# x of two more blocks transposed by the DMA queue, the first up step in halves, and a new set of dates for the order

## The chip, the cores and the metric

The kernel runs on one core of one Trainium2 chip. The metric is the device time of one execution in microseconds (us), the median of several runs. A profiled execution has a span (first to last instruction of the program) and its own time, which is a little longer.

## What is computed

Attention with a local window and a few global keys, and behind it a gated feed-forward layer. Batch 4, 8 heads, 768 positions, 64 elements a head; window 96, 8 global keys; 3072 tokens of 512 elements, 2048 hidden.

```python
scores = scale * np.matmul(q, k.transpose(0, 1, 3, 2))
is_global = pos[None, :] < int(n_global)
is_local = (rel >= 0) & (rel < int(n_local))
dist = np.where(is_global & ~is_local, float(n_local), np.abs(rel))
scores = scores - slopes[:, None, None] * dist          # slope 2**-(h+1) of head h
scores = np.where(is_global | is_local, scores, -1000000000.0)
a = np.exp(scores - np.max(scores, axis=-1, keepdims=True))
a = a / (np.sum(a, axis=-1, keepdims=True) + 1e-09)
x = np.matmul(a, v)                                     # heads side by side: 3072 x 512
h = x @ w_in                                            # 512 x 2048
out = (h * (1.0 / (1.0 + np.exp(-1.702 * h)))) @ w_out  # 2048 x 512
```

All data are float32. The kernel keeps the precision by splitting a factor into a high and a low half of 16 bits and adding three products (high x high, high x low, low x high).

## The kernel before

**Tiling.** The tokens are 24 blocks of 128 rows; two blocks make a chunk of 256 rows, so there are 12 chunks. Blocks 0 to 3 are the first 128 positions of each of the four batches (`EARLY = 4`, `place`); a window never leaves such a block, and they are treated apart (`prep_first`, `first`). Blocks 4 to 23 look back at the block before them (`prep`, `unit`, four units of two heads each).

**Attention of blocks 0 to 3.** `load` fetches q and k, 256 KB each. `turn` transposes them on TensorE, four float32 transposes of 128x128 each into a PSUM bank (`tq`, line 485). `taken` evicts them, scaled, to `QZ` (queries, with zeros that `clean` writes into the other half) and `KF` (keys; line 492). `scores` (lines 672 and 673) multiplies them and adds the mask, VectorE takes the maxima (line 677), a small transpose (line 680) and a copy (line 681) bring them into place, the transposed scores follow (lines 692 to 698), an exponential on ScalarE (line 710) and the products with v (line 704). `weigh_first` (lines 739 to 743) divides and writes `x` of the block.

**x for the feed-forward layer.** `finish` makes two 16-bit halves of x, transposed. For blocks under `TURN_X` TensorE transposes x into PSUM (line 763, four transposes a block), ScalarE casts the high half (line 766) and VectorE subtracts for the low half (line 767). For the others, the halves are made first, in `x16` (lines 771 and 773), and one DMA transpose on SP's queue brings both into place (line 774). `x_ready[n]` is the last of these tasks.

**The feed-forward layer.** w_in and w_out come in eight steps each (`weights(s, u)`): a load of 1 MB (line 242) and five operations of VectorE and ScalarE (lines 420 to 426) that split it into halves. For chunks 0 and 1, `up(c, s)` multiplies a chunk with a step of w_in: 24 matmuls with 256 moving columns (line 861), then tanh and the gate on ScalarE and VectorE (lines 870 to 873). `down(c, s)` multiplies with w_out and accumulates in PSUM (line 969). Chunks 2 to 11 use `up_two` and `down_two`, a scheme with seven in place of eight products over two steps (line 901), for which `twist` prepares sums of the weights and `sums` sums of x.

**What sets the order.** Every piece of work is a task: the engines it can run on with a duration each, the tasks it comes after, the buffers it uses, and a due time. `Work.order` runs once when the program is built. It passes due times back along the dependencies, adds the entry of `NUDGE` for the task's tag (`tag` for engines, `tag` with an "l" for tasks of SP's queue), and then plays the engines and the DMA queue through in a planned time: a free engine takes the ready task with the earliest due time whose buffers are free. A task isn't looked at until `AHEAD` = 24 us before it is due, or until its own `soon`. A DMA is planned as 1.95 us of latency, its duration on the one queue and 0.9 us to land. The result is a fixed order of instructions for each engine; on the chip each engine works in that order and waits for semaphores. Durations and dates have no other effect than on this order and on the choice of the engine. Where TensorE would have nothing to do in the first `WARM` = 50 us of planned time, the planner puts in a filler, a matmul of ones that nobody reads (`spare`, line 1147); fillers use the ring of banks `r_h`, and so do the transposes `tq` of blocks 1 to 3 and the up steps.

**Buffers.** A `Ring` has a number of buffers under one tag. A `Buf` takes the next one; in rings that are not `loose` they are taken in the order in which they were declared. PSUM has eight banks: `r_s` 1, `r_pv` 1, `r_h` 2, `r_y` 4. `r_x16` has one buffer, which holds the masks (`mk`) at first.

**Masks.** From two small integers (window and number of global keys) a matmul (`cs`, line 392) and some VectorE operations make the masks: `M1` for a block's own keys (line 385, 128x128), then `m2` and `M2` for the keys of the block before (lines 375 to 377, and 383 or 385 with 128x256), which are first used by block 4.

Of the kernel before, what the change touches and what calls it, by code (L numbers as in the profile page):

```python
# [8 lines left out]
F32 = mybir.dt.float32  # L9
# [10 lines left out]
P = 128  # L20
# [8 lines left out]

NUDGE = {"M2": -8.8, "T2": 21.9, "T3": 11.2, "block1": 2, "block10u2": -2.7, "block10u2l": -0.5,  # L30
# [37 lines left out]
NG = 8  # L68
SKIP = 24
EARLY = 4  # L70

FIRST = 4
LAST = 0.9365
TURN_X = 4
WARM, GAP = 50.0, 0.5
AHEAD = 24.0
BACKLOG = 3.0
TWO = 3
LAT = 0.2
MM128, MM256, MM512, MM64, FP128, FP65, TURN = 0.056, 0.109, 0.216, 0.029, 0.264, 0.21, 0.11  # L80
# [165 lines left out]
def kernel(  # L246
# [11 lines left out]
    nc = tc.nc  # L258
# [1105 lines left out]
```

## Time and profile before

| | us |
|---|---|
| median of 3 runs | 588.26 (587.92 to 588.53) |
| the profiled execution | 587.09 |
| its span | 585.2 |
| TensorE (PE) busy | 577.2 |
| VectorE (DVE) busy | 497.1 |
| ScalarE (ACT) busy | 461.5 |

An engine is counted as busy from the start to the end of each of its instructions; matmuls overlap in the pipeline and their ends are modelled, so that a following matmul's start tells more than an end. PEld is the loading of weights, which overlaps with matmuls. "Idle" is the time of an engine ahead of an instruction, and the profile names what ended it. SP only issues DMAs and waits; its transfers run on 16 DMA engines that all queues share. A row of a timeline merges instructions of one kind that follow each other.

### The profile page before, as it was taken

The page shows a single profiled execution, that of the slowest core. Times are in us where ns is not written, and L with a number is a line of the kernel's source. Part 1 is how long each engine was busy: PE and PEld are TensorE (multiplying, and loading weights), DVE is VectorE, ACT ScalarE, POOL GpSimd, SP SyncE. Part 2 cuts the span into 40 slices and gives each one's busy share as a digit, 9 for nine tenths or more (in the row PEclk, how much of TensorE's full clock was granted, in tenths as well). Part 3 has the DMA queues.
Part 4 walks back from the last instruction along what each step waited for, and adds up shares of the span by engine and source line. Part 5 has one row for each costly group of instructions (what it writes and reads, how often), then busy time and mean ns, then how long its engine had stood idle before and what let it go on. Part 6 is the DMA issues. An engine that isn't in the chain of part 4 may idle for free. (4 is left out here: it accounts for less than half of the span.)

```text
span 585.2 us, 16904 instructions
## 1 busy us (share of the span) xinstructions
PE 577.2 (99%) x6744; PEld 435.0 (74%) x6744; DVE 497.1 (85%) x1180; ACT 461.5 (79%) x1086; POOL 3.7 (1%) x14
## 2 busy tenths in 40 slices
PE   8999999999999999999999999999999999999997
PEld 5886766677668678778679767777777866876896
DVE  7898999999999999888899699889889878775462
ACT  6778899898678979888798798788987878874351
POOL 2000000000000000000000000000000000000000
PEclk9999999999999999999999999999999999999999
DMA  9998998987667787989999998999998899970101
GB/s 259 299 295 215 312 227 244 207 202 144 166 145 147 146 154 163 215 162 198 226 183 194 200 222 207 200 219 189 247 202 189 203 204 227 196 182 19 37 2 41
DMA packets 268265, 109.57 MB, mean 187 GB/s; under 512 B 249300, under 2 KB 249812, under 8 KB 268180
## 3 DMA queue, kind: packets, MB, share of 16 engines
q1 hardware_dynamic: 268032, 108.30, 83.3%
q8 instruction: 54, 0.88, 0.7%
q14 instruction: 31, 0.25, 0.1%
q10 hardware_dynamic: 148, 0.13, 0.1%
HBM read 57.67 MB, written 6.29 MB: 109 GB/s over the span
## 5 line engine op out<-in xcount | busy, mean ns | idle before, releaser
L969 PE MATMUL y<-w,g 128*128 128x512 f16 (+1 forms) x1248 | 264.9, 363 | 0.2
L969 PEld LDWEIGHTS <-g 128*128 128x128 f16 x1248 | 118.0, 98 | 106.3 <-DVE g L873 1.0
L901 PEld LDWEIGHTS <-w 128*128 128x128 f16 x1728 | 101.4, 98 | 3.9
L615 ACT ACTIVATE p<-p,NM 128x232 f32<-128x232 f32 x160 | 76.3, 479 | 9.4 <-DVE NM L605 9.3
L901 PEld LDWEIGHTS <-T 128*128 128x128 f16 x1296 | 76.8, 98 | 5.2 <-issue 0.2
L861 PE MATMUL h<-xT,w 128*128 128x256 f16 x576 | 67.2, 273 | 0.2 <-DVE t L871 0.2
L605 DVE CUSTOM_DVE_ANT_0 p<-s,mm 128x232 f32<-128x232 f32 x160 | 57.5, 393 | 9.8 <-PE s L599 9.5
L861 PEld LDWEIGHTS <-w 128*128 128x128 f16 x576 | 55.4, 98 | 8.1 <-DVE t L871 0.3
L942 DVE SCALAR_TENSOR_TENSOR g<-t,g 128x512 f16<-128x512 f32 x72 | 49.0, 685 | 11.8 <-ACT g L941 11.6
L620 DVE TENSOR_TENSOR hl<-p,hl 128x464 f16<-128x464 f32 x80 | 50.7, 635 | 5.1 <-ACT hl L619 4.8
L941 ACT ACTIVATE g<-t 128x512 f16<-128x512 f32 x72 | 44.9, 628 | 12.4 <-PE y L969 8.5
L933 ACT ACTIVATE t<-h 128x512 f32<-128x512 f32 (+1 forms) x72 | 35.8, 517 | 18.3 <-DVE h L909 16.6
L619 ACT CAST hl<-p 128x464 f16<-128x464 f32 x80 | 46.0, 575 | 2.2 <-DMA pt<-hl 0.8
L909 DVE TENSOR_TENSOR h<-pb,h 128x256 f32<-128x256 f32 x72 | 28.4, 418 | 19.6 <-PE pb L901 17.3
L901 PE MATMUL pa<-xS,T 128*128 128x128 f16 x648 | 44.8, 219 | 0.0
L599 PEld LDWEIGHTS <-QK 128*128 128x128 f16 x640 | 36.5, 98 | 5.8 <-DVE NM L605 1.7
L934 DVE SCALAR_TENSOR_TENSOR t<-t,h 128x512 f32<-128x512 f32 (+1 forms) x72 | 38.4, 550 | 2.3 <-ACT t L933 2.0
L599 PE MATMUL s<-QK 128*128 128x128 f16 x320 | 38.2, 219 | 0.0
L901 PE MATMUL pa<-xT,w 128*128 128x128 f16 x540 | 37.5, 219 | 0.0
L901 PE MATMUL pb<-xS,w 128*128 128x128 f16 x540 | 37.5, 219 | 0.0
L632 PE MATMUL pv<-VR,pt 128*128 128x64 f16 x288 | 34.5, 193 | 0.0
L631 PE MATMUL pv<-VR,pt 128*128 128x64 f16 x288 | 34.5, 193 | 0.0
(186 smaller groups left out, 1030.2 us busy)
## 6 DMA issues: line engine op xcount, KB each, us to landing
ws<-in_moe_w_in_dram SPq DMA_DIRECT2D x8, 1024.0 KB
ws<-in_moe_w_out_dram SPq DMA_DIRECT2D x8, 1024.0 KB, 5.7
raw<-in_q_dram SPq DMA_DIRECT2D x24, 256.0 KB, 4.2
raw<-in_k_dram SPq DMA_DIRECT2D x24, 256.0 KB, 5.3
QK<-QK SPq DMA_DIRECT2D x40, 128.0 KB, 5.4
raw<-in_v_dram SPq DMA_DIRECT2D x20, 256.0 KB, 3.2
out_dram<-yo SPq DMA_DIRECT2D x20, 256.0 KB
ws_00again<-in_moe_w_in_dram SPq DMA_DIRECT2D x8, 512.0 KB, 3.8
```

Of the source, the lines that this page charges most:

```text
L599: nc.tensor.matmul(sp()[:, j, lo:hi], d["QK"]()[:, 0, h, :], K[:, 1 + z, h, P - (hi - lo):], start=(z == 0), stop=(z == 1), skip_group_che ...
L605: nc.vector.tensor_tensor_reduce(out=pr()[:, j, :], in0=sp()[:, j, :], in1=m, scale=-1.0 / SC, scalar=3.0e38, op0=ALU.add, op1=ALU.min, ac ...
L615: ex.append(add({"ACT": 0.473}, lambda e, j=j: nc.scalar.activation(pr()[:, j, :], pr()[:, j, :], AF.Exp, bias=NM[:, n, hs[j]:hs[j] + 1], ...
L619: t4 = add({"ACT": 0.5}, lambda e: nc.scalar.copy(hl()[:, 0, :, SKIP:], pr()), ex, [pr, hl])
L620: t5 = add({"DVE": 0.55}, lambda e: nc.vector.tensor_sub(hl()[:, 1, :, SKIP:], pr(), hl()[:, 0, :, SKIP:]), [t4], [pr, hl])
L861: nc.tensor.matmul(ph()[:, fi, :], w1(s, cc, z, fi), X[:, y, cc, :], start=(j + cc == 0), stop=(j == 2 and cc == NCC - 1))
L901: nc.tensor.matmul(o()[:, fi], w, x()[:, y * NCC + 2 * k + cc, t], start=(first and fi + j + cc == 0), stop=(last and j + cc == 3), skip_g ...
L933: t1 = add({"ACT": 0.06 + 0.22 * w}, lambda e: nc.scalar.activation(o(), src(), AF.Tanh, scale=0.851 / (SX * SW)), after, srcs)
L934: return add({"DVE": 0.08 + 0.265 * w}, lambda e: nc.vector.scalar_tensor_tensor(o(), o(), 1.0, src(), ALU.add, ALU.mult), [t1], srcs)
L941: t4 = add({"ACT": 0.53}, lambda e, g=g, tt=tt: nc.scalar.mul(g()[:, 0], tt(), SG / (SX * SW)), u, [tt, g])
L942: t5 = add({"DVE": 0.61}, lambda e, g=g, tt=tt: nc.vector.scalar_tensor_tensor(g()[:, 1], tt(), SG / (SX * SW), g()[:, 0], ALU.mult, ALU.s ...
L969: nc.tensor.matmul(y(), part(zg, f), w2(s, z, f % 2)[:, m], start=(begin and f + j == 0), stop=(end and j == 2 and f == 2 * len(steps) - 1 ...
```

## The change

- `TURN_X` goes from 4 to 2: x of blocks 2 and 3 (chunk 1) goes through `x16` and the DMA transpose.
- `HALVES = 1`: `up(0, 0)` is issued as four tasks in place of two, each with 12 matmuls of 128 columns, one for each block of the chunk and each half `fi` of the step; a task waits only for its own block's `x_ready`.
- `turns`: the transposes `tq` of block 1 get the banks `r_y[0, 1]` and `r_pv`; those of block 0 keep `r_y[1, 0]` and `r_y[1, 1]`.
- `clean`: the zeros of blocks 1 and 2 are POOL's, those of blocks 0 and 3 ScalarE's (before: 0 and 1 ScalarE's, 2 and 3 POOL's), with other due times; block 3's is not looked at before 12 us of planned time.
- `m2` and `M2` are not looked at before 12 us of planned time.
- The planner's durations of loads, DMA transposes, `counts` and the small matmul `cs` are other ones.
- All entries of `NUDGE` are replaced.
- The first buffers of `r_VF`, `r_KG` and `r_pr` are allocated ahead of the others.

```diff
-NUDGE = {"M2": -8.8, "T2": 21.9, "T3": 11.2, "block1": 2, "block10u2": -2.7, "block10u2l": -0.5,
...
+NUDGE = {"T0": -17.4, "T1": -25.4, "again": 11.6, "block10u0": -0.2, "block10u3": 16.8, "block11u0": 1.5,
...
-TURN_X = 4
+TURN_X = 2
...
+HALVES = 1
...
-    m1 = add({"DVE": 0.55}, counts, [m0], want=0.0)
-    m1 = add({"PE": 0.12}, lambda e: nc.tensor.matmul(cs(), each, one, start=True, stop=True), [m1], [cs])
+    m1 = add({"DVE": 1.0}, counts, [m0], want=0.0)
+    m1 = add({"PE": 0.6}, lambda e: nc.tensor.matmul(cs(), each, one, start=True, stop=True), [m1], [cs])
...
+    for t in (m2, *M2):
+        t.soon = 12.0
...
-        t0 = add({"SP": 2.75}, lambda e: load_weights(nc, ws(), w_in, w_out, s, u), bufs=[ws])
+        t0 = add({"SP": 2.5}, lambda e: load_weights(nc, ws(), w_in, w_out, s, u), bufs=[ws])
...
-        return [add({"SP": 1.2 if n < 2 and 2 not in parts else 1.35}, lambda e, z=z: nc.sync.dma_start(
+        return [add({"SP": 0.95}, lambda e, z=z: nc.sync.dma_start(
...
-        zero = add({"ACT": 1.2} if n < 2 else {"POOL": 1.2}, clean, bufs=[QZ], want=-10.0 if n < 2 else 1e9)
+        zero = add({"POOL": 1.1} if n in (1, 2) else {"ACT": 1.25}, clean, bufs=[QZ], want=(-10.0, 0.0, 1e9, 1e9)[n])
+        if n == 3:
+            zero.soon = 12.0
...
-            tq = Buf(r_y[1, z] if n == 0 else r_h, [P, NU, P], F32, f"tq{n}_{z}")
+            tq = turns.get((n, z)) or Buf(r_h, [P, NU, P], F32, f"tq{n}_{z}")
...
-            add({"SP": 1.2 if n < 2 else 1.35}, lambda e: nc.sync.dma_start(
+            add({"SP": 1.0}, lambda e: nc.sync.dma_start(
...
-        t3 = add({"SP": f * 2.8}, lambda e: nc.sync.dma_start_transpose(
+        t3 = add({"SP": f * 2.1}, lambda e: nc.sync.dma_start_transpose(
...
-        t6 = add({"SP": 0.7 * ns}, lambda e: nc.sync.dma_start_transpose(pt(), hl().rearrange("p a h w -> p (a h w)")),
+        t6 = add({"SP": 0.55 * ns}, lambda e: nc.sync.dma_start_transpose(pt(), hl().rearrange("p a h w -> p (a h w)")),
...
+    turns = {(n, z): Buf(r, [P, NU, P], F32, f"tq{n}_{z}") for n, z, r in
+             ((0, 0, r_y[1, 0]), (0, 1, r_y[1, 1]), (1, 0, r_y[0, 1]), (1, 1, r_pv))}
...
-        t4 = add({"SP": 1.4}, lambda e: nc.sync.dma_start_transpose(xT[c]()[:, :, t, :], x16().rearrange("p a m -> p (a m)")),
+        t4 = add({"SP": 1.1}, lambda e: nc.sync.dma_start_transpose(xT[c]()[:, :, t, :], x16().rearrange("p a m -> p (a m)")),
...
-        def mms(e, fi):
+        def mms(e, fi, at):
...
-                    nc.tensor.matmul(ph()[:, fi, :], w1(s, cc, z, fi), X[:, y, cc, :],
+                    nc.tensor.matmul(ph()[:, fi, at], w1(s, cc, z, fi), X[:, y, cc, at],
...
-        t1 = ups[c, s] = [add({"PE": 12 * MM256}, lambda e, fi=fi: mms(e, fi), [x_ready[2 * c], x_ready[2 * c + 1], W_ready[s, 0]],
-                  [ph, xT[c], WT[s, 0]], want + 1.3 * fi) for fi in range(2)]
+        pieces = [(slice(0, TC), (0, 1))] if c or s >= HALVES else [(slice(t * P, t * P + P), (t,)) for t in range(2)]
+        t1 = ups[c, s] = [add({"PE": 12 * MM256 / len(pieces) + 0.018 * (len(pieces) - 1)}, lambda e, fi=fi, at=at: mms(e, fi, at),
+                              [*(x_ready[2 * c + t] for t in ts), W_ready[s, 0]], [ph, xT[c], WT[s, 0]], want + 1.3 * fi)
+                          for at, ts in pieces for fi in range(2)]
...
+    for r in (r_VF, r_KG, r_pr):
+        r.line[0]()
```

73 rows, old and new, of the table NUDGE are left out of this document.

## The prediction

> **What bounds the kernel now.** I read the page first, then busy time by stretches with the filler matmuls of line 1147 apart, then TensorE's timeline up to 51 us, and last the groups that the change touches. From the page:
>
> ```profile
> span 585.2 us, 16904 instructions
> PE 577.2 (99%) x6744; PEld 435.0 (74%) x6744; DVE 497.1 (85%) x1180; ACT 461.5 (79%) x1086; POOL 3.7 (1%) x14
> ```
>
> TensorE is busy for 99% of the span. The chain of waits says nothing here (one piece, the last ScalarE instruction), so I look for the stretches in which TensorE does no useful work. Columns: stretch, length, busy time (and instructions) of PE, PEld, DVE, ACT, POOL, clock, DMA share, GB/s. Behind it, the same for the filler matmuls alone.
>
> ```profile
> 0.00:4.91 4.91, 3.58 (x11) 1.22 (x11) 2.79 (x15) 3.29 (x5) 3.68 (x14) 1.00 0.63 143
> 4.91:14.57 9.66, 8.87 (x82) 6.75 (x82) 8.27 (x29) 6.72 (x12) 0.00 (x0) 1.00 1.07 317
> 14.57:21.44 6.87, 6.87 (x65) 6.30 (x62) 5.58 (x12) 5.37 (x7) 0.00 (x0) 1.00 0.90 198
> 21.44:26.27 4.83, 3.73 (x38) 3.08 (x38) 4.70 (x11) 3.30 (x7) 0.00 (x0) 1.00 1.01 384
> 26.27:45.00 18.73, 18.73 (x178) 16.66 (x176) 17.04 (x27) 13.93 (x20) 0.00 (x0) 1.00 1.00 302
> 45.00:60.00 15.00, 15.00 (x105) 10.15 (x104) 13.69 (x22) 12.07 (x14) 0.00 (x0) 1.00 0.85 214
> 60.00:130.00 70.00, 69.28 (x638) 48.80 (x636) 68.19 (x140) 64.88 (x137) 0.00 (x0) 1.00 0.96 240
> 130.00:581.30 451.30, 451.10 (x5644) 342.01 (x5642) 376.85 (x929) 351.45 (x889) 0.00 (x0) 1.00 0.82 170
> ...
> 4.91:26.27 21.36, 1.85 (x7) 0.59 (x6) 1.00 1.00 294
> ```
>
> So the time splits into four: 4.91 us ahead of the first useful matmul; a start up to 26.27, in which 1.85 us is filler and 0.79 + 1.10 = 1.89 us is idle, 3.74 us in all; a body of 555 us in which TensorE idles 0.72 + 0.20 = 0.92 us; and a tail of 3.9 us behind the last matmul. Only three things can make the kernel faster: less TensorE work, less of the 4.91 + 3.74, less of the 0.92. The edits reach no further than that, about 7 us; there is no such floor under a loss. The second thing to see is VectorE: 17.04 of 18.73, then 68.19 of 70 us busy. It converts the weights, and what is put on it late stays late for long.
>
> **The change part by part.** TensorE's timeline around the start (start us, us, instruction):
>
> ```profile
> 5.21 0.66 PE L485 MATMUL tq<-ident,raw 128*128 128x128 f32 x4
> 5.71 0.81 PE L1147 MATMUL idle<-idle 128*128 128x512 bf16 x3
> 6.36 0.60 PE L485 MATMUL tq<-ident,raw 128*128 128x128 f32 x4
> 7.79 0.22 PE L672 MATMUL s<-hl,QZ 128*128 128x128 bf16 x1
> 8.69 0.60 PE L485 MATMUL tq<-ident,raw 128*128 128x128 f32 x4
> 9.17 0.38 PE L1147 MATMUL idle<-idle 128*128 128x512 bf16 x1
> 10.54 0.22 PE L672 MATMUL s<-hl,QZ 128*128 128x128 bf16 x1 [0.31 <-ACT hl L492]
> 22.75 0.65 PE L763 MATMUL tx<-ident,x 128*128 128x128 f32 x4 [0.27 <-DVE x L743]
> 25.27 0.66 PE L485 MATMUL tq<-ident,raw 128*128 128x128 f32 x4 [0.83 <-ACT QZ L492]
> 26.27 1.47 PE L861 MATMUL h<-xT,w 128*128 128x256 f16 x12
> 27.58 0.27 PE L680 MATMUL aux<-ident,top 128*8 128x128 f32 x1
> 47.39 0.60 PE L763 MATMUL tx<-ident,x 128*128 128x128 f32 x4
> 47.82 2.75 PE L969 MATMUL y<-w,g 128*128 128x512 f16 x12
> 50.41 2.78 PE L861 MATMUL h<-xT,w 128*128 128x256 f16 x24
> ```
>
> *x of blocks 2 and 3 by the queue.* Four transposes occupy TensorE from 47.39 to 47.82, 0.43 us; two blocks are 0.87 us. The last filler is the one at 9.17, so what is freed there is used by the next matmul: −0.87 (bounds 0, if it only turns into idle time, and −0.87). On ScalarE and VectorE almost nothing changes, since a cast and a subtraction stay, from SBUF in place of PSUM:
>
> ```profile
> L766 ACT CAST xT<-tx x4: 580/585/585, 20.0 to 48.0; 128x512 f16<-128x512 f32 x4
> L771 ACT CAST x<-x x13: 602/614/620, 96.7 to 526.1; 128x512 f16<-128x512 f32 x13
> L773 DVE TENSOR_TENSOR x<-x,x x20: 678/684/693, 98.2 to 527.1; 128x512 f16<-128x512 f32 x20
> L774 SPq DMA_TRANSPOSE xT<-x x20: 1233/1314/3387, 108.0 to 527.8; - x20
> DMA to landing us min/median/max: 4.3/4.9/5.7
> 46.42 0.21 DVE L743 TENSOR_TENSOR x<-aux,sm 128x64 f32<-128x64 f32 x1
> 49.44 0.67 DVE L767 TENSOR_TENSOR xT<-tx,xT 128x512 f16<-128x512 f32 x1
> ```
>
> What changes is when chunk 1 is there. Now x of block 3 is written at 46.42 + 0.21 = 46.63 and its transposed halves at 50.11; the up step that begins at 50.41 fits to that, and I take it for chunk 1's first. By the queue, 0.61 + 0.68 + 4.9 = 6.2 us lie between, so from the same x it would be 52.8, 2.7 us later. Queued behind the two transposes on SP are weight and key loads, 1.3 us of issuing for each; SP and the DMA engines have room there (the DMA share is 0.85 in 45 to 60). I cost the 2.7 us at nothing because attention of block 3 can be put ahead of chunk 0's second and third up steps, 2 x 2.62 us of TensorE work that the trace has in front of it; if the new order doesn't, this is the first rival's loss.
>
> *First up step in halves.* Twelve matmuls of 256 columns take 27.58 − 26.27 = 1.31 us, so the step 2.62. In halves it is 48 matmuls of 128 columns. Of lines 672 and 673 sixteen such matmuls, each with a weight load of its own, run from 7.79 to 8.69, 0.056 us each: 48 x 0.056 = 2.69, +0.07 (that each loads its own weights excludes a dearer price). Its first half needs block 0 alone. The waits of 0.27 and 0.83 us at 22.75 and 25.27, 1.10 us, can then be covered by 1.3 us of up work, if block 0's x and the first weight are ready by 22:
>
> ```profile
> L426 DVE SCALAR_TENSOR_TENSOR w<-wa,w x5: 1212/1215/1227, 16.3 to 39.1; 128x1024 f16<-128x1024 f32 x5
> 20.57 0.69 DVE L767 TENSOR_TENSOR xT<-tx,xT 128x512 f16<-128x512 f32 x1 [0.70 <-ACT xT L766]
> 8.62 1.28 DVE L677 TENSOR_REDUCE top<-s 128x4 f32<-128x512 f32 x2
> 9.81 1.29 DVE L385 TENSOR_SCALAR mm<-mk 128x256 bf16<-128x256 f32 x6
> 9.14 0.72 ACT L383 ACTIVATE mm<-mk 128x256 bf16<-128x256 f32 x2
> ```
>
> They are: the first of the five conversions up to 50 us ends at 16.3 + 1.2 = 17.5, the halves of x at 20.57 + 0.69 = 21.26. −1.1 (bounds 0 and −1.1).
>
> *Masks later, own banks, zeros on other engines, true durations.* These go together: they decide how the remaining 4.91 + 2.64 us shrink. ScalarE does 0.72 us of masks for block 4 and later (line 383) just ahead of the eviction that the scores at 10.54 wait for; not before 12 us in the planner's time, they leave that wait. VectorE's maxima (line 677) start at 8.62, behind three mask operations, while the first four heads' scores (half of the sixteen products) are through near 8.24; they move up a little. Block 1's first transposes no longer share banks with the fillers. With loads costed at 0.95 us and not 1.2, block 0's keys are taken about 0.6 us earlier than 6.36. I take −0.8 of the 2.64 and −0.3 of the 4.91 (bounds 0 and −2.6; 0 and −1.2). Block 0's products now also wait for a bank that block 1's transposes hold; that bank is read by 10.5, and these products start at 14.57, so it costs nothing, with 4 us of cover. The 1.29 us of line 385 and some 0.8 us ahead of it move into a stretch in which VectorE has 18.73 − 17.04 = 1.69 us free: bounds 0 and +2.1 on the weights, taken as 0 because TensorE has chunk 1's steps to do meanwhile. One zero fill moves from ScalarE to POOL and one the other way, off the path.
>
> The new costs are near what the queue does. A weight load is 1,048,576 bytes, a load of q, k or v 262,144:
>
> ```profile
> 23.00:28.00 5.00, 4.17 (x44) 3.58 (x43) 4.18 (x8) 3.88 (x6) 0.00 (x0) 1.00 1.03 410
> 30.00:31.50 1.50, 1.50 (x15) 1.21 (x14) 1.50 (x3) 1.50 (x2) 0.00 (x0) 1.00 1.11 253
> ```
>
> At 410 GB/s a weight takes 2.56 us (now costed 2.5, before 2.75); at 253 GB/s a load takes 1.04 (now 0.95). The Trainium skill speaks against the new figure: on its page "DMA: Bandwidth & Descriptors", section "Where 436 GB/s comes from", the memory side binds a transfer from HBM at about 358 GB/s. By that a weight takes an estimated 2.93 us, the five weights that are converted before 50 us would be 5 x 0.43 = 2.1 us later than costed, and the sum would end 2.1 us higher. The row of 410 GB/s disagrees with it, and the measurement decides.
>
> *Dates anew.* All the dates by which the order is made are replaced. This adds and removes no work; it can only change idle time. The body has 0.92 us of it, so the gain ends at −0.9. A loss has no row; nearest is the worst stretch of before, 0.72 us in 70, and four times that, +2.9 us, is my bound above. I take 0, since with costs nearer to the traced ones I see no reason for a worse body.
>
> **Sum:** −0.87 + 0.07 − 1.1 − 0.8 − 0.3 + 0 = −3.0 us. The profiled execution took 587.09, its span and 1.9 us around it: 584.1. The median of the runs shown is 588.26, 1.17 above it; on that scale the forecast is **585.2**, with a range of its own of 583.0 to 587.0.
>
> **The rivals.** *Chunk 1 comes late (slower).* TensorE reaches the step at 50.41 some 3.0 us earlier, at 47.4, and finds chunk 1 landed only at 52.8 if block 3's x stays at 46.63: 5.4 us idle, −3.0 + 5.4 = +2.4, 590.7. For it: only five weights are converted by then (the row of line 426), so chunk 0's work is used up. Against it: attention of block 3 can go in front, which costs nothing. It decides from the x of block 3: as early as 41.2 the gain is whole, later than 44.2 it is gone, and from 45.4 on the kernel is slower by over 0.2%. By the Trainium skill's page "TensorE: Matmul & The Clock Gate", section "HAM oscillation — how this bites in real kernels", idle gaps of over about 3.4 us also halve the clock for a while; the longest gap behind the first useful matmul is 0.83 us and the clock 1.00, so no run shows it.
>
> *VectorE takes it back (no change).* TensorE arrives 3 us earlier at 60 to 130 us, where VectorE is 97% busy, and waits for scores and conversions there: idle grows from 0.7 to about 3.5 us, time 588.0. For it: that stretch's waits are on VectorE (the row below), and the masks moved 2 us of VectorE work towards it. Against it: later blocks' attention can give way.
>
> ```profile
> PE s L599 <- DVE NM L605: 0.5, 2, 0.3
> ```
>
> *The start shrinks more.* All of the 3.74 us and 0.9 of the 4.91 go: −0.8 − 3.7 − 0.9 = −5.4, 582.8. Against it: block 0's chain of evictions leaves TensorE little to do before 12 us.
>
> *The change doesn't do what it says.* The freed 0.87 us and the halves only turn into filler, which the planner may place up to 50 us: −0.3 − 0.8, 587.2. Filler behind 10 us would show it; before has none there.
>
> **How the numbers follow.** The forecast has 0.56, the larger gain 0.08, VectorE 0.13, filler 0.07, late chunk 0.16. This measurement can tell about 0.2%, 1.2 us, from no change: 587.1 to 589.4. The forecast's own range and the larger gain lie below it; of filler 0.03 does too. Faster 0.67, same 0.17, slower 0.16. The range, 582.4 to 589.2, reaches over the larger gain and over the two cases of no change, and leaves out most of the late chunk and 0.04 below.
>
> **What would show it.** Right: fillers and idle time between the first useful matmul and 26 us fall from 3.7 to under 2; the first 128-column up matmuls run near 20 us; line 763 has 8 instructions, not 16; block 3's x is written before 42; idle time in 60 to 130 us stays near 0.7. Wrong: a wait of TensorE for the transposed x between 45 and 55 us, or waits on VectorE of over 3 us behind it, would each overturn the sum.

## The result, and the profile after

The kernel with the change takes 605.08 us (600.92 to 607.76, six runs); the kernel before, on the same chip, 588.39 (587.44 to 589.43). The ratio is 1.0277, 95% interval 1.0241 to 1.0314: 16.7 us slower, where 585.2 was forecast and 589.2 was the upper end of the range. The profiled execution took 603.95 us.

From the page of the profile after:

```profile
span 602.2 us, 16916 instructions
PE 579.8 (96%) x6757; PEld 434.8 (72%) x6757; DVE 496.7 (82%) x1175; ACT 462.4 (77%) x1091; POOL 3.7 (1%) x14
q1 hardware_dynamic: 270144, 108.82, 82.3%
```

Nearly the same work, 17.0 us longer: the last ScalarE instruction, which reads the last matmul, starts at 598.29, before at 581.37. The windows after, cut where those of before were cut (first useful matmul, up step of chunk 0, and so on), with the fillers' own window row last:

```profile
0.00:4.72 4.72, 3.39 (x8) 1.28 (x9) 2.73 (x15) 2.54 (x3) 3.69 (x14) 1.00 0.60 137
4.72:26.30 21.58, 18.05 (x154) 14.55 (x153) 17.94 (x47) 16.01 (x27) 0.00 (x0) 1.00 1.01 314
26.30:45.00 18.70, 18.57 (x199) 16.27 (x199) 17.20 (x28) 14.32 (x20) 0.00 (x0) 1.00 1.04 274
45.00:60.05 15.05, 12.81 (x82) 7.92 (x81) 12.07 (x19) 10.88 (x15) 0.00 (x0) 1.00 1.12 275
60.05:130.00 69.95, 67.65 (x596) 47.66 (x595) 65.19 (x122) 60.67 (x118) 0.00 (x0) 1.00 0.87 211
130.00:598.30 468.30, 459.33 (x5722) 347.07 (x5722) 381.60 (x949) 357.51 (x912) 0.00 (x0) 1.00 0.81 168
...
4.72:26.30 21.58, 1.94 (x6) 0.49 (x5) 1.00 1.01 314
```

TensorE's idle time (length less the first busy figure) is 3.53 us in the start, where it was 1.89; then 0.13, 2.24, 2.30 and 8.97, 13.6 us in the body, where it was 0.92. That is 14.4 of the 17.0 us; the other 2.6 stand in TensorE's busy figure. An estimate of mine fits that: the trace has 32 gaps between matmuls, before 11, and a matmul of 128 columns ahead of a gap is counted with its whole 0.22 us, where the next one would start after 0.056; 21 x 0.16 = 3.4, less some 0.8 us of work that the change takes away. The loss has no one place: it is spread over the body.

What TensorE waits for, in the view of its waits (line <- what released it: us in total, times, longest):

```profile
PE pv L636 <- DMA pt<-hl: 6.4, 10, 1.1
PE h L869 <- DVE t L881: 1.3, 1, 1.3
PE h L869 <- DMA xT<-x: 1.1, 1, 1.1
...
PE s L605 <- DMA QK<-QK: 0.7, 1, 0.7
```

First come waits for `pt`, the exponentials that the DMA queue brings back transposed (line 627). The view of that tile gives what all engines that use it waited for; of its 15.0 us after, 6.4 are matmuls and 8.6 are TensorE's weight loads, which overlap with matmuls. Here is its row after; before, this list holds no DMA, only the second row:

```profile
  DMA pt<-hl: 15.0, 22
```

```profile
  PE sT L698: 2.1, 4
```

So data that the order counted on come late from the queue. Direct waits of matmuls for a DMA (`pt` 6.4, x 1.1, queries and keys 0.7, values 0.3) are 8.5 of the 13.6 us; the others name VectorE or ScalarE, and how many of these go back to a late transfer wasn't followed. What a late transfer does beyond its own wait is seen at chunk 1 (VectorE's, SP's and TensorE's timelines after):

```profile
53.10 0.21 DVE L751 TENSOR_TENSOR x<-aux,sm 128x64 f32<-128x64 f32 x1
54.50 0.69 DVE L424 TENSOR_SCALAR w<-ws 128x1024 int32<-128x1024 int32 x1 [1.18 <-DMA ws<-in_moe_w_in_dram]
55.11 1.22 DVE L430 SCALAR_TENSOR_TENSOR w<-wa,w 128x1024 f16<-128x1024 f32 x1
56.24 0.69 DVE L781 TENSOR_TENSOR x<-x,x 128x512 f16<-128x512 f32 x1
...
56.95 1.23 SPq L782 DMA_TRANSPOSE xT<-x  x1
...
60.05 3.22 PE L869 MATMUL h<-xT,w 128*128 128x256 f16 x28 [1.13 <-DMA xT<-x]
```

Block 3's x is written at 53.31, but the subtraction for its low half starts only at 56.24 (line 781): VectorE's order has a weight's first operation (line 424) ahead of it, and that stands 1.18 us for its load. The transpose goes out at 56.95, and TensorE, which had nothing to do with that weight, waits 1.13 us at 60.05.

### The profile page after: what moved, and what is told of

Read it like the earlier page. It is cut to its first block, busy times and chain, and to the rows that moved or that the text cites. A ratio compares the mean times of both kernels' runs of the same rounds, so it can differ in the third digit from the quotient of the medians.

```text
span 602.2 us, 16916 instructions
## 1 busy us (share of the span) xinstructions
PE 579.8 (96%) x6757; PEld 434.8 (72%) x6757; DVE 496.7 (82%) x1175; ACT 462.4 (77%) x1091; POOL 3.7 (1%) x14
## 5 line engine op out<-in xcount | busy, mean ns | idle before, releaser
L869 PE MATMUL h<-xT,w 128*128 128x256 f16 (+1 forms) x600 | 68.5, 268 | 4.3 <-DVE t L881 1.3
L943 ACT ACTIVATE t<-h 128x512 f32<-128x512 f32 (+1 forms) x72 | 36.0, 516 | 18.7 <-DVE h L919 17.9
L636 PE MATMUL pv<-VR,pt 128*128 128x64 f16 x288 | 34.2, 193 | 5.6 <-DMA pt<-hl 5.3
L636 PEld LDWEIGHTS <-pt 128*128 128x128 f16 x320 | 29.2, 98 | 12.1 <-DMA pt<-hl 8.6
```

Source lines behind the costliest of these rows:

```text
L636: nc.tensor.matmul(o, ph, V[:, 0, h], start=(s == 0), stop=False, skip_group_check=True)
L869: nc.tensor.matmul(ph()[:, fi, at], w1(s, cc, z, fi), X[:, y, cc, at], start=(j + cc == 0), stop=(j == 2 and cc == NCC - 1))
```

## The experiments

**How they are read.** The kernel's `order` gives a planned time for each task when the program is built, and so a planned end of the last matmul. That is no time of a chip, but it says what the order counts on. On the chip that end is taken as the start of ScalarE's last instruction less 0.1 us (in the kernel before 581.37 − 0.1 = 581.3; planned 581.0). Chip less plan is called slip. The kernel before has a slip of 0.3 us, the changed kernel one of 598.2 − 584.2 = 14.0. My theory after the traces: the order counts on more than the queue gives (MARGIN below). Its rivals: the new set of dates is at fault, or the changed structure, or SP's issuing.

| kernel | planned end | on the chip | slip | median us | ratio to before (95%) |
|---|---|---|---|---|---|
| before | 581.0 | 581.3 | 0.3 | 588.4 | |
| after | 584.2 | 598.2 | 14.0 | 605.1 | 1.028 (1.024 to 1.031) |
| e1 change, no dates | 580.1 | 614.2 | 34.1 | 623.2 | 1.060 (1.057 to 1.064) |
| e2 before, new DMA durations | 583.7 | 604.3 | 20.6 | 611.3 | 1.040 (1.037 to 1.043) |
| e3 before, no dates | 584.3 | 587.1 | 2.8 | 593.4 | 1.009 (1.006 to 1.012) |
| e4 change, old durations and dates | 587.7 | 591.9 | 4.2 | 598.2 | 1.017 (1.014 to 1.020) |
| e5 before, short transposes | 583.5 | 589.3 | 5.8 | 595.4 | 1.013 (1.010 to 1.016) |
| e6 before, short loads | 584.2 | 599.4 | 15.2 | 606.4 | 1.033 (1.030 to 1.036) |
| e7 change, old durations, no dates | 585.6 | 591.2 | 5.6 | 597.2 | 1.014 (1.011 to 1.017) |
| e8 as e1, fewer bytes | 580.1 | 604.7 | 24.6 | 608.8 | 1.033 (1.027 to 1.038) |
| e9 before, short q, k, v | 585.9 | 604.6 | 18.7 | 611.0 | 1.038 (1.035 to 1.041) |
| e10 change, old durations, dates searched | 581.9 | 592.9 | 11.0 | 598.7 | 1.017 (1.015 to 1.019) |
| e11 the same, searched with a margin | 582.5 | 593.2 | 10.7 | 598.8 | 1.016 (1.014 to 1.019) |
| e12 change, longer durations, no dates | 595.9 | 594.3 | −1.6 | 599.9 | 1.020 (1.016 to 1.023) |
| e13 before, dates searched | 581.1 | 589.8 | 8.7 | 594.6 | 1.011 (1.007 to 1.015) |
| e14 change, all DMAs x1.15, dates searched | 588.2 | 589.7 | 1.5 | 596.2 | 1.014 (1.011 to 1.016) |
| e15 before, all DMAs x1.15, dates searched | 587.4 | 589.7 | 2.3 | 595.5 | 1.013 (1.011 to 1.014) |

"No dates" is `NUDGE = {}`. The six durations are those of the weights (`t0`), of q, k and v (two places) and of the DMA transposes `t3` (queries and keys), `t6` (`pt`) and `t4` (x). Differences below are against runs of the kernel before on the same chip (587.8 to 589.0 us).

**Are the dates at fault, or the durations?** e1 is the changed kernel with

```diff
-NUDGE = {"T0": -17.4, "T1": -25.4, "again": 11.6, ...
+NUDGE = {}
```

> The changed kernel with no dates of its own (NUDGE empty): queue transposes, halves, banks, masks and the new durations stay. The order's own planned end of the last matmul is 580.1 us, for the changed kernel it is 584.2 and for the kernel before 581.0; on the chip those two ended at 598.3 and 581.3. Theory MARGIN (the new, shorter DMA durations leave the plan without slack, so that in-order engines stand at DMAs that land after their planned time): about as many body waits as in the changed kernel, end 8 or more us past the plan, median 592 to 600. Theory DATES (this one set of dates is at fault): the end is within 3 us of the plan, body idle below 3 us, median 586 to 589. Theory STRUCTURE (x of chunk 1 by the queue, halves and banks cost it): waits for xT between 45 and 60 us and a median near 590 whatever the dates.

It is slower still, 623.18 us, 23 above the range that MARGIN gave: that is 34.6 us over before, the change 16.7. So with these durations the new dates gain 17.9 us over none. The plan of e1 (e8 has the same) is the shortest of all, 580.1, and misses by the most. The tile `pt` in it:

```profile
  DMA pt<-hl: 35.7, 23
```

e2 is the kernel before, its dates too, with the new values of the six durations alone:

```diff
-        t0 = add({"SP": 2.75}, lambda e: load_weights(nc, ws(), w_in, w_out, s, u), bufs=[ws])
+        t0 = add({"SP": 2.5}, lambda e: load_weights(nc, ws(), w_in, w_out, s, u), bufs=[ws])
-        return [add({"SP": 1.2 if n < 2 and 2 not in parts else 1.35}, ...      # q, k: 0.95;  v: 1.0
-        t3 = add({"SP": f * 2.8}, ...                                           # 2.1
-        t6 = add({"SP": 0.7 * ns}, ...                                          # 0.55
-        t4 = add({"SP": 1.4}, ...                                               # 1.1
```

> The kernel before, its dates and structure kept, with only the planner's DMA durations (loads 0.95 and 1.0, weights 2.5, transposes 2.1, 1.1 and 1.1) taken from the change; no instruction differs but the order. Planned end of the last matmul 583.7 us. Theory MARGIN: end 6 or more us past the plan, median 595 to 602, TensorE waits for pt, QK or VR by DMA of over 4 us. Theory DATES: within 3 us of the plan, median 589 to 593. Theory STRUCTURE: as DATES.

611.26 us, 22.7 more than before and 9 above MARGIN's range, though only the order is another (with it the engine of some operations, and the fillers). The wait for `pt` comes first among TensorE's waits in e2, as in the changed kernel:

```profile
PE pv L630 <- DMA pt<-hl: 5.5, 9, 1.5
PE pa L901 <- ACT h L917: 3.2, 4, 1.4
```

e3 takes the dates from the kernel before and leaves its durations:

```diff
-NUDGE = {"M2": -8.8, "T2": 21.9, "T3": 11.2, ...
+NUDGE = {}
```

> The kernel before with its old, longer DMA durations and no dates (NUDGE empty). Planned end of the last matmul 584.3 us. Theory MARGIN: as with the kernel before, the end is within 2 us of the plan, median 590 to 593, hardly a wait for a DMA. Theory DATES: within 3 us of the plan too if no dates are harmless, but far behind it (over 6 us) if it is dates that keep DMAs from being late.

593.42 us: the dates of before are worth 4.9 us, and without them the plan still holds to 2.8 (MARGIN said 2, and 590 to 593 us; both are passed by less than 1). Both kernels without dates, the one slips 2.8 and the other 34.1 us, so the lack of fitted dates alone doesn't make an order slip.

**What is left of the change without the durations?** e4 is the change with the six durations and the dates of before; e7 with the six durations of before and no dates.

```diff
 e4: the six durations and NUDGE of the kernel before, in the changed kernel
 e7: the six durations of the kernel before, and
+NUDGE = {}
```

> The changed kernel's structure (queue transposes for blocks 2 and 3, halves, banks, masks, zeros, the durations of the two small mask operations) with the old DMA durations and the old dates. Planned end of the last matmul 587.7 us. Theory MARGIN: within 2.5 us of the plan, median 594 to 597, hardly a wait for a DMA behind 60 us. Theory STRUCTURE: 4 or more us past the plan, with waits for xT at 45 to 60 us. Theory DATES: within 3 us of the plan.

> The changed kernel's structure with the old DMA durations and no dates; planned end of the last matmul 585.6 us. It differs from the kernel before without dates (planned 584.3, on the chip 587.2, median 593.4) by the structure alone, and from the changed kernel without dates (planned 580.1, on the chip 614.3, median 623.2) by the six DMA durations alone. Theory MARGIN: within 5 us of the plan, median 592 to 598, and 25 us or more below the run with the new durations. Theory STRUCTURE: 8 or more us past the plan, waits for xT or for VectorE of over 4 us before 60 us, median above 600.

598.15 and 597.17 us; the dates of before do nothing for the changed kernel. Both slips are larger than MARGIN said (4.2 for 2.5, 5.6 for 5), and e4's is one that STRUCTURE named, though TensorE has no wait for a DMA of x in it. Giving the old durations back takes 25.6 us off e1 (34.6 and 9.1 over before), and the tile `pt` falls to

```profile
  DMA pt<-hl: 5.0, 10
```

These four make a path from before to after, each step one edit: dates of before taken out +4.9 (e3), the other parts of the change +4.2 (e7), the new durations +25.6 (e1), the new dates −17.9 (after). That they add up to 16.7 is no test, since each is a difference of two neighbours. And it is one path of several. By the runs e13 and e10 below, which have searched dates, it reads: other dates for the kernel before +6.9 (e13), the other parts of the change with dates searched in the same way +2.9 (e10), from there to the change, with its durations and its own dates, +7.0. So the new durations cost 22.7 us in the kernel before, with its dates, and 25.6 in the changed one without dates; but of the 16.7 us, with dates that go with them, their part may be as little as 7.

**Which durations?** On the kernel before, with its dates: e5 shortens the three transposes alone, e6 the loads of weights, q, k and v, e9 those of q, k and v.

```diff
 e5
-        t3 = add({"SP": f * 2.8}, ...
+        t3 = add({"SP": f * 2.1}, ...
-        t6 = add({"SP": 0.7 * ns}, ...
+        t6 = add({"SP": 0.55 * ns}, ...
-        t4 = add({"SP": 1.4}, ...
+        t4 = add({"SP": 1.1}, ...
 e6
-        t0 = add({"SP": 2.75}, ...
+        t0 = add({"SP": 2.5}, ...
 e6 and e9
-        return [add({"SP": 1.2 if n < 2 and 2 not in parts else 1.35}, ...
+        return [add({"SP": 0.95}, ...
-            add({"SP": 1.2 if n < 2 else 1.35}, ...
+            add({"SP": 1.0}, ...
```

> The kernel before with its dates, and of the new durations only those of the DMA transposes (2.1, 1.1, 1.1 in place of 2.8, 1.4, 1.4 us); nothing but the order differs. Planned end of the last matmul 583.5 us. With all new durations (the run before this one) the kernel ended at 604.1, 20.4 past its plan. Theory TRANSPOSES (the 256-byte packets of transposes are what the queue can't do in the planned time): 12 or more us past the plan, median above 601. Theory LOADS (q, k, v and weights are): under 6 us past it, median below 596.

> The kernel before with its dates, and of the new durations only those of the loads (weights 2.5 in place of 2.75, q, k and v 0.95 and 1.0 in place of 1.2 and 1.35 us). Planned end of the last matmul 584.2 us. Theory TRANSPOSES: under 6 us past the plan, median below 597. Theory LOADS: 12 or more us past it, median above 602.

> The kernel before with its dates, and of the new durations only those of q, k and v (0.95 and 1.0 in place of 1.2 and 1.35 us); weights and transposes keep the old ones. Planned end of the last matmul 585.9 us. All loads short: planned 584.2, on the chip 599.5, 15.3 past it. Theory QKV (a load of 256-byte packets is what is underrated, 68 of them through the body): 10 or more us past the plan, median above 602. Theory WEIGHTS (the sixteen of 1 MB ahead of 110 us): under 6 us past it, median below 599.

595.44, 606.41 and 610.99 us: +7.3, +18.3 and +22.0. The loads of q, k and v alone make as much of the loss as all six together (22.7), so the parts don't add up; the new figure for a weight isn't needed for it (with it, e6 is shorter than e9). Nor does the sum of what a plan asks of the queue rank the slips: it is 418.0 us in e5, 423.8 in e6 and 427.8 in e9, while they slip 5.8, 15.2 and 18.7. It matters which transfers are planned too short. In e9 TensorE waits for `pt` again, and for queries and keys from the queue:

```profile
PE pv L630 <- DMA pt<-hl: 6.5, 5, 2.5
...
PE s L599 <- DMA QK<-QK: 2.9, 2, 2.1
```

**Is it the queue's bytes, or SP's issuing?** SP needs 1.23 us or more to issue a transpose (1.26 in the median for `pt`, in e1), and it issues in order too. e8 has e1's order, task for task, and as many DMAs; only the 32 second loads of weights, from which sums of squares are formed, fetch 64 KB in place of 512 KB each.

```diff
-    nc.sync.dma_start(ws.rearrange("p (c f) t -> p c (f t)", c=n), ...
+    nc.sync.dma_start(ws[:, 0:few], words[0:P, 0:2 * few].rearrange("p (f t) -> p f t", t=2))     # few = 64
```

> The changed kernel without dates (median 623.2, planned end 580.1, real 614.0; TensorE idle 5.3 us in 265 to 400 and 11.2 in 400 to 530, 16.5 together, of which 13.8 is waits for pt) with one edit that leaves its order as it is: the 32 second loads of the weights (512 KB each, from 265 us on) bring 64 KB each, and the check that reads them works on those; so 14 of 110 MB and seven eighths of that check are left out, while the instructions, their number and their lengths on ScalarE, VectorE and SP stay. Theory BYTES (the queue can't move what the plan asks of it in the planned time): the DMA share in 265 to 530 falls from 0.94 to about 0.75, idle there from 16.5 to under 5 us, median 604 to 612. Theory ISSUE (it is the time that SP takes to issue a DMA, 1.26 us a transpose and about 0.57 a load, and the latency of each, that the plan misses): idle there stays above 13 us, median 618 or more.

608.83 us, 13.6 nearer to before than e1. The windows of e1 and then of e8 in which those loads lie:

```profile
265.00:400.00 135.00, 129.67 (x1666) 97.34 (x1664) 111.08 (x281) 113.15 (x291) 0.00 (x0) 0.99 0.94 194
400.00:530.00 130.00, 118.85 (x1542) 88.61 (x1540) 104.54 (x263) 102.73 (x269) 0.00 (x0) 1.00 0.94 203
```

```profile
265.00:400.00 135.00, 129.84 (x1701) 97.73 (x1699) 113.14 (x290) 114.02 (x294) 0.00 (x0) 1.00 0.82 152
400.00:530.00 130.00, 129.99 (x1683) 97.32 (x1682) 113.19 (x285) 109.99 (x291) 0.00 (x0) 1.00 0.74 158
```

In 400 to 530 us TensorE's idle time falls from 11.15 to 0.01 us, with the DMA share from 0.94 to 0.74. In 265 to 400 us it stays (5.33 and 5.16), though the share falls there too. So in the second window it is the time that transfers take on the shared queue, not the number of issues, which is the same; for the first this leaves it open, and the idle time of 5.2 us over both is just above the 5 that BYTES named.

**Does more room on the queue take the slip away?** e12 is e7 with the six durations some 15% longer:

```diff
-        t0 = add({"SP": 2.75}, ...                    +3.15
-        q and k 1.2, v and later blocks 1.35          +1.4, 1.55
-        t3, t6, t4: 2.8, 0.7, 1.4                     +3.2, 0.8, 1.6
```

> The change with no entries in NUDGE and the six DMA durations of the kernel before made about 15% longer (weights 3.15, q, k and v 1.4 and 1.55, transposes 3.2, 0.8 and 1.6 us); nothing of the work differs. The order's own plan ends its last matmul at 595.9 us, against 580.1 with the new durations and 585.6 with those of before (both without dates), where the chip ended 34 and 5.7 us behind the plan. MARGIN (an order that asks the queue for more than it gives slips, because each engine keeps its order behind a late DMA): a third dose, so the slip falls to 3 us or less, TensorE's waits for pt (the exponentials brought back transposed) to under 1 us in sum (16.2 and 1.6 in those two), median between 601 and 606 us. BOUND (the DMA engines themselves are what cannot go faster, whatever the order asks): the waits on DMAs stay as with the durations of before, and the median is within 1.5 us of 597. SCATTER (the slip has nothing to do with the durations; any order without fitted dates misses by some amount): a slip anywhere between 5 and 30 us, median 608 to 632.

The slip is gone, the chip is 1.6 us ahead of the plan, and neither the waits of TensorE nor the tile `pt` list a wait for `pt` any more. The median of 599.87 lies 1.1 below the range given for MARGIN, for the chip beat the plan. So three doses of the same structure without dates, planned shorter, as before, and longer, slip 34.1, 5.6 and −1.6 us. The room has its own price: the plan is 10.3 us longer than e7's, the time 2.7. How much room it is shows against the trace: the plan of e12 asks 520.4 us of the queue, which took 0.802 x 598.3 = 480, so it has 8% more than needed, where e7's has 466.3 for 0.837 x 595.3 = 498, 6% less.

**Why do searched dates not hold?** With the old durations, dates were found by altering `NUDGE` at random and keeping what made the plan shorter: for the plan as it is (e10), and for the mean of the plans with DMAs at 1.0 and 1.15 times their durations (e11). The edit is another `NUDGE` in e7.

> The changed kernel's structure (x of blocks 2 and 3 by the queue, halves, banks, masks) with the old DMA durations and dates searched anew for the shortest planned end under these durations: last matmul planned at 581.9 us, against 584.2 of the changed kernel and 581.0 of the kernel before. Theory BYTES (an order made with the queue's real load keeps its plan): on the chip within 6 us of the plan, median 589 to 595, at least 10 below the changed kernel. Theory STRUCTURE (queue transposes, halves and banks lose whatever the order): 10 or more past the plan, median above 598. If the structure brings what was forecast, 588 or less.

> As the run before, but the dates are searched for the mean of two plans, one with the old DMA durations and one with all of them 15% longer; built with the old durations, last matmul planned at 582.5 us. Theory BYTES, with slack worth having: fewer waits for DMAs than in the run before, within 3 us of the plan, median 588 to 592. Theory STRUCTURE: as the run before, above 598.

Both missed what BYTES said and fall where STRUCTURE put them: slips of 11.0 and 10.7, and 598.7 and 598.8 us, no better than with no dates (+9.7 and +9.8; e7 +9.1). Two causes were open, the changed structure and the fitting. e13 puts dates searched as in e10 on the kernel before; e14 and e15 plan every DMA of SP 1.15 times as long and search dates under that, for the changed structure and for that of before.

```diff
 e14, e15, in Work.order
-                t, us = best, best.on[e]
+                t, us = best, best.on[e] * (1.15 if e == "SP" else 1.0)
```

> The kernel before with its own durations and another set of NUDGE, found as for e10_change_old_durations_new_search (dates altered at random, kept where the order's own plan came out shorter). The plan ends its last matmul at 581.1 us, as the dates of before do (581.0). STRUCTURE (the 11 us by which the changed kernel missed its plan there come from the changed structure): here the plan holds as it did for before, slip under 3 us, median 588 to 591. FITTED (a plan made as short as it will go by its dates misses on the chip, whatever the structure; that the dates of before hold theirs comes from more than the plan): slip 7 to 15 us, median 595 to 603.

> The change, durations of before, every DMA planned 1.15 times as long, and dates searched for the shortest plan under these longer DMAs; it ends its last matmul at 588.2 us. MARGIN: with room on the queue even a searched plan holds: slip under 3 us, TensorE's waits for pt under 1 us in sum, median 592 to 598. FITTED without regard to the queue: slip 7 to 15 us as in e10, median 602 to 610. In neither case does it beat the kernel before (588.4).

> The kernel before with every DMA planned 1.15 times as long and dates searched for the shortest plan under that; it ends its last matmul at 587.4 us, 0.8 ahead of e14_change_longer_durations_new_search. MARGIN: slip under 3 us, median 591 to 597. STRUCTURE (the changed structure costs something by itself): e14 is longer than this one by more than 3 us; if the structure is neutral, by 0 to 2 us.

e13 slips 8.7 us on the structure of before, whose own dates give as short a plan (581.1 and 581.0) and slip 0.3. Its median, 594.62, is 0.4 below FITTED's range, yet far from STRUCTURE's 588 to 591: fitting to the plan alone can be enough for a slip of this size. (It is one set of dates; another could slip more or less. Some 2.8 of the 8.7 us are a lower clock of TensorE after early waits, as the last section works out.) With the longer DMAs the searched plans hold, 1.5 and 2.3, in the ranges given. And e14 is 0.8 us longer than e15, within the spread of their runs (594.4 to 596.9 and 594.8 to 595.8): with room on the queue no cost of the changed structure is seen, where it was 4.2 without dates, and no gain in either. Here are TensorE's two longest waits in e13, for values of a global key and for `pt`, both from the queue, and then the two longest in e14, where no DMA is among the waits:

```profile
PE pv L594 <- DMA VR<-VG: 2.1, 1, 2.1
PE pv L594 <- DMA pt<-hl: 1.4, 3, 0.7
```

```profile
PE s L568 <- DVE NM L574: 2.6, 3, 1.3
PE s L568 <- DVE QKover L515: 1.7, 1, 1.7
```

Open is what the dates of before have that searched ones lack; the plan doesn't show it, and how they were found isn't on record. No version came below the kernel before.

## Why the prediction was wrong, step by step

**The step that failed** is "The new costs are near what the queue does", and with it "Dates anew", taken as 0 and bounded by +2.9. The durations were taken as estimates that get better when they come nearer to a traced one. e2 shows what they are (22.7 us lost by them alone): an order that counts on shorter transfers asks for data sooner than they come, and each engine stands in its fixed order behind them. e13 shows that dates too can't be put at nothing: other ones cost the kernel before 6.9 us. The body's idle time went from 0.92 us to 13.6 in the changed kernel; four times the worst stretch of before was no bound, since a stretch of before says nothing of an order that asks for more. How the 16.7 us divide between durations and dates stays open, as the two paths above show.

The two rows were also read wrongly. 410 and 253 GB/s are rates of 5 and 1.5 us in which the queue had one kind of work (by the packet records, 745 packets of 2 and 4 KB and almost no others in the first, 1,421 of 256 bytes in the second), at shares over 1. Over the body the kernel before has

```profile
26.00:520.00 494.00, 493.10 (x5850) 367.69 (x5848) 443.70 (x1034) 418.59 (x1005) 0.00 (x0) 1.00 0.93 203
```

203 GB/s at a share of 0.93, 218 at a full one, all kinds together. Summed by size over the whole trace of before, the packets of 256 bytes, which are those of q, k and v and of the transposes among others, took 334.5 us of the 16 engines for 61.9 MB, 185 GB/s; those of 2 and 4 KB, the weights among them, took 147.2 us for 46.0 MB, 313 GB/s. By that, an estimate, a load of q, k or v takes 262,144 / 185 = 1.42 us, where the kernel before plans 1.2 (q and k of the first two blocks) or 1.35 and the change 0.95 or 1.0; and a weight 1,048,576 / 313 = 3.35 us, where they plan 2.75 and 2.5. The new costs went away from these, not towards them; e12's (1.4, 1.55 and 3.15) are nearest. The whole queue could have been held against the plan in the same way. From the page of before:

```profile
q1 hardware_dynamic: 268032, 108.30, 83.3%
```

0.833 x 585.2 = 487 us of transfers. The durations of all of SP's tasks add up to 463.5 us in the plan of before, 5% less; in the plan of the change to 380.5, against 0.823 x 602.2 = 496 on the chip, 23% less. The three shorter transposes were not costed at all; alone they make +7.3 us (e5).

What spoke for small transfers being dear stood on the page of before:

```profile
DMA packets 268265, 109.57 MB, mean 187 GB/s; under 512 B 249300, under 2 KB 249812, under 8 KB 268180
```

93% of the packets are under 512 bytes. The Trainium skill's page "DMA: Bandwidth & Descriptors" has a section "Why small descriptors are slow (HBM only)", by which a piece of 256 bytes, as q, k and v are fetched in here, spends 27% on overhead. The trace agrees in direction (185 GB/s in packets of 256 bytes, 313 in larger ones; 253 and 410 in the prediction's two rows). The prediction passed over this rule, which bore on the loads that mattered. It did weigh that page's limit of 358 GB/s for the weights, and set it aside for the row of 5 us; over the whole trace 313 GB/s is nearer to that limit than to 410, though what holds the rate there no run shows, and e6 against e9 shows that the loss doesn't need the weights' figure.

**x of blocks 2 and 3 by the queue, −0.87.** TensorE does 8 of these transposes in place of 16:

```profile
L771 PE MATMUL tx<-ident,x x8: 272/273/329, 21.2 to 25.2; 128*128 128x128 f32 x8
```

The work went, as said. The rival's late chunk 1 came in part: it was put at 5.4 us, and the wait at 60.05 is 1.13. The room that the prediction saw on the queue in 45 to 60 us (a share of 0.85) isn't there after the change: the share is 1.12.

**Halves, +0.07 and −1.1.** The gain failed on its condition, block 0's x and the first weight "ready by 22". TensorE's, VectorE's and ScalarE's timelines after:

```profile
23.41 1.04 PE L491 MATMUL tq<-ident,raw 128*128 128x128 f32 x8
24.78 0.66 PE L771 MATMUL tx<-ident,x 128*128 128x128 f32 x4 [0.33 <-DVE x L751]
26.30 1.50 PE L869 MATMUL h<-xT,w 128*128 128x128 f16 x24 [0.86 <-ACT QZ L498]
27.64 0.22 PE L680 MATMUL s<-hl,QZ 128*128 128x128 bf16 x1
...
18.43 1.22 DVE L430 SCALAR_TENSOR_TENSOR w<-wa,w 128x1024 f16<-128x1024 f32 x1
20.61 0.21 DVE L751 TENSOR_TENSOR x<-aux,sm 128x64 f32<-128x64 f32 x1
20.74 2.35 DVE L427 SCALAR_TENSOR_TENSOR wa<-ws,w 128x1024 int32<-128x1024 int32 x2
23.01 0.68 DVE L775 TENSOR_TENSOR xT<-tx,xT 128x512 f16<-128x512 f32 x1
...
22.08 0.57 ACT L774 CAST xT<-tx 128x512 f16<-128x512 f32 x1
24.45 0.71 ACT L385 ACTIVATE mm<-mk 128x256 bf16<-128x256 f32 x2
25.07 1.18 ACT L498 ACTIVATE QZ<-tq 64x512 f32<-64x512 f32 x2
```

and VectorE's before, where block 0's x is written:

```profile
18.53 0.21 DVE L743 TENSOR_TENSOR x<-aux,sm 128x64 f32<-128x64 f32 x1
```

The size was right: 24 matmuls take 27.64 − 26.30 = 1.34 us, 0.056 each. The weight is ready at 19.65, but the halves of block 0's x only at 23.69, 2.4 us later than in the kernel before (21.26). Most of that is older than the halves: x itself is written at 20.82, before at 18.74. The two conversions on VectorE (line 427), which end at 23.09, add at most 0.4 us, for the high half is there at 22.65. At 23.69 both banks of `r_h` hold the transposes issued at 23.41, and ScalarE evicts them after 0.71 us of the masks that were moved: the first half starts at 26.30, the whole step before at 26.27. The two waits that it was to cover are there as before, 0.33 and 0.86 for 0.27 and 0.83. The prediction asked when data would be ready in the order of before; the order was made anew, and a bank was needed too.

**Start, −0.8 and −0.3.** The first useful matmul is 0.19 us earlier (4.72 for 4.91). The rest didn't come: filler and idle time up to the first up matmul are 1.94 + 3.53 = 5.47 us, before 3.74, where under 2 was named as the sign.

**The other signs.** Block 3's x is written at 53.31, not before 42. Idle time in 60 to 130 us is 2.3, not 0.7; the VectorE rival had 3.5 there, but not for its reason: VectorE is busy for 65.2 us of that stretch, in the kernel before for 68.2. None of the rivals had the cause, so neither its price nor its chance was in the range. The sum itself, 588.26 − 3.0, is 585.3 and not 585.2, which changes nothing.

## What to carry to other kernels

Where an order is fixed when the program is built, the durations it is made with are promises, and in-order engines pass a broken promise on. Cost each kind of transfer on a shared queue at its rate over the whole trace (here 185 GB/s in small packets and 313 in larger ones, not 253 and 410), and compare what the plan asks of the queue with what it takes in the trace (here 380 against 496 us). That sum is a warning and no price: e5 asks for less than e9 and slips less. Before a change of such numbers is costed at nothing, or dates are fitted to a plan, see how far the plan and the chip lie apart. Here plans with durations some 15% above those of before held to about 2 us, and plans fitted to those of before missed by 9 to 11; yet none of the plans that held was faster than the kernel before, whose plan has no such room and holds.

## What the runs showed of the hardware

The clock of TensorE fell after waits, but not in the kernel before nor in the changed one (the granted clock of both is 1.00 up to the last matmul, in windows of 1 us). TensorE's timeline in e8, and then its windows (the clock is the third figure from the end):

```profile
32.99 2.72 PE L835 MATMUL h<-xT,w 128*128 128x256 f16 x12 [4.44 <-DVE top L651]
```

```profile
30.00:40.00 10.00, 7.01 (x40) 5.11 (x40) 8.24 (x11) 6.75 (x10) 0.00 (x0) 0.66 1.01 333
40.00:50.00 10.00, 10.00 (x99) 8.74 (x97) 9.19 (x16) 9.53 (x16) 0.00 (x0) 1.00 0.89 252
```

After a wait of 4.44 us twelve matmuls took 2.72 us, where they take 1.47 in the kernel before, and the granted clock of that stretch is 0.66. So this wait cost 1.25 us more than its length, in these twelve alone. e1, which has the same order, waits 4.24 us there, and its clock in the same window is 0.83. The prediction said that no run shows the rule of the Trainium skill's page "TensorE: Matmul & The Clock Gate", section "HAM oscillation — how this bites in real kernels"; this run agrees with it. The length of one wait doesn't settle it, though: in e7 the clock is 0.50 from 33 to 36 us after a wait of 2.46, and twelve such matmuls take 2.50 us; in e12 it stays at 1.00 after one of 2.70.

Summed over windows of 1 us, what the clock lacks is 1.71 us in e2, e4, e6, e7, e12 and e15, two times that in e9, e11 and e13, three times in e1, four times in e8, and nothing in before, the change, e3, e5, e10 and e14: as much as 3.4 us at half clock each time. By an estimate from the same windows, weighted by TensorE's busy share, this is 2.8 of the 8.7 us that e13 slips and 5.0 of e1's 34.1; the 14.0 of the change have none of it.

And kernels that slipped far also spread further from run to run, if loosely: 1.9 to 7.0 us from the shortest to the longest time in the nine that slip by more than 8 us (600.9 to 607.8 for the change), 0.7 to 2.5 in the five others that slip by less than 5. The kernel before, with up to 11 runs on one chip, spreads up to 3.3.
